# First MLP: the second product moved two slices behind the first, with a third activation buffer and a reordered weight conversion

## The chip, the cores and the metric

The kernel runs on one core of a Trainium2 chip. The metric is device time in microseconds (us) of one execution. The engines are TensorE (PE; its weight loads are listed apart as PEld), VectorE (DVE), ScalarE (ACT), GpSimd (POOL) and SyncE (SP), which here issues every DMA. Each engine runs its own instructions strictly in the order in which they are written, so an instruction that waits holds up all that stand behind it on its engine.

## What is computed

Cross-attention between 512 positions and 32 state rows (8 batches, 8 heads, head size 64) gives 8 x (512 + 32) = 4352 rows of 512. Two MLPs follow, 512 to 2048 to 512 each; the inputs are float32.

```python
xread = softmax(scale * x @ state.T) @ state          # 512 rows per batch
sread = softmax(scale * state @ x.T) @ x              # 32 rows per batch
x = concat([xread, sread])                            # 4352 rows of 512
h = x @ w_in;  g = max(h, 0) + alpha * min(h, 0);  x = g @ w_out      # first MLP
h = x @ w_in2; g = h - tanh(h);                    out = g @ w_out2   # second MLP
```

The weights arrive as 64-bit words and are converted on the core. Each float32 operand of a product is split into a high and a low part, and a product is three matmuls (high x high, high x low, low x high: `TERMS`).

## The kernel before

The first MLP goes through nine blocks of rows: batches 0 to 6, then the small block of all 256 state rows, then batch 7. Each block has 16 slices `f` of 128 hidden columns. For one slice:

- `emit_h` is the **first product**: 12 matmuls of 512 columns in block 0 (weights `wi`), 6 in blocks 1 to 7, where the weights were first multiplied by the state (`pw`), and 12 of 256 columns in the small block. It writes one of two PSUM banks, `ps_h`.
- `act_a` is three steps in a row: ACT writes `t` (L599), DVE rewrites `ps_h` in place from `ps_h` and `t` (L600), ACT writes the high part of `g` (L601). `act_b` is DVE's low part of `g` (L605), the last reader of the `ps_h` bank.
- `emit_o` is the **second product**: 12 matmuls into four accumulators `acc`, which a block holds from its slice 0 to its slice 15. After slice 15 `finish` copies them out to four tiles `y` (two by ACT at L629, two by DVE at L631) and `store` issues their DMAs (L638) at the end of the loop step.

The loop runs the second product one slice late: in step `f` PE gets the first product of `f`, then the second product of `f - 1`. So `finish` of a block falls into step 0 of the next one.

Between these, a timetable written out by hand (`plan`, filled by `at`) places everything else at five points of a step ("early" and "gap" around `act_a`, "mid" ahead of the second product, "late" behind it, "end"): the attention of the next batch, the projections of weights by the state for later blocks (`project`, L367, and `project_one`, L397: three matmuls into `ps_p`, ACT's copy `ph`, DVE's remainder `pl`, and DMAs of both), and, from block 3 on, the conversion and combination of the second MLP's weights (`combining`; stores `wc`). Projections, attention and state transposes share two PSUM banks (`ps_a`). In block 0 the first MLP's own weights are converted: 32 jobs, each half of a pair (w_in of slice f, w_out of slice f), that pass through `conv_load` to `conv_d`, one phase per `tick`; the list `jobs` sets their order. The SBUF pool `work` gives buffers by tag: `g`, `t` and `y` have two each, `sc` and `at` one.

```python
    jobs = [(f, half) for f in range(NF) for half in range(2)]
...
                y = work.tile([P, S], F32, tag="y", name="y")[:, :n]
...
                if pend:
                    emit_o(*pend)
```

Of the kernel before, what the change touches and what calls it, by code (L numbers as in the profile page):

```python
# [12 lines left out]
F32 = mybir.dt.float32  # L13
F32R = mybir.dt.float32r
# [8 lines left out]
P = 128  # L23
# [12 lines left out]
def attention_and_two_mlps(ctx, tc, x, state, w1_in, w1_out, alpha, w2_in, w2_out, out):  # L36
    nc = tc.nc
    B, H, S, D = x.shape
    NS = state.shape[2]
    DM = H * D  # L40
# [3 lines left out]
    NF = DFF // P  # L44
    NC = S // P
    GH = P // NS
    NG = H // GH
    NP = GH // 2
    HP = 2 * NS
    FQ = DM // P  # L50
# [5 lines left out]
    work = tc.alloc_tile_pool(name="work", bufs=2)  # L56
    w_outs = tc.alloc_tile_pool(name="w_outs", bufs=NF // FQ)
# [39 lines left out]
    def w_out(f, part):  # L97
        return WO[f // FQ][:, part, f % FQ, :]
# [22 lines left out]
    def low_word(q, r):  # L121
        nc.scalar.activation(q, r[:, :, 0].bitcast(U32), AF.Copy, scale=2.0**-29)

    jobs = [(f, half) for f in range(NF) for half in range(2)]
    raws, words, low, loaded = {}, {}, {}, set()

    def conv_load(k):
# [160 lines left out]
    xraw, SG = {}, {}  # L288

    def load_state(b, g, tag="sg"):  # L290
        sg = work.tile([P, D], F32, tag=tag, name=f"{tag}{b}_{g}", bufs=4)
        nc.sync.dma_start(out=sg, in_=state[b, g * GH:(g + 1) * GH].rearrange("h n d -> (h n) d"))
        SG[(b, g) if tag == "sg" else (b, g, 0)] = sg

    def load_x(b, g):
        if b < 2:
            load_state(b, g)
        if b == 0:
            if g == 0:
                xraw[b] = w_outs.tile([P, 2 * NC * GH * D], F32, tag="wo", name="xr0")  # L300
            n = NC * GH * D
            t = xraw[b][:, g * n:(g + 1) * n].rearrange("p (c h d) -> p c h d", c=NC, h=GH)
        else:
            t = work.tile([P, NC, GH, D], F32, tag="xr", name=f"xr{b}_{g}")
        for h in range(GH):
            nc.sync.dma_start(out=t[:, :, h, :],
                              in_=x[b, g * GH + h].rearrange("(p c) d -> p c d", c=NC))
        xraw[b, g] = t
# [12 lines left out]
    def lead(b):  # L321
        return b if b % 2 or b == B - 1 else b - 1
# [105 lines left out]
    def attention(b, g, spare=False):  # L428


        st = {}

        def psum(shape, name):
            if spare:
                return ps_acc.tile(shape, F32, tag="acc", name=name)
            return ps_a.tile(shape, F32, tag="a", name=name)

        def wide_tile(tag, other):
            if spare:
                return work.tile([P, S], F32, tag=other, name=tag)  # L440
            return work.tile([P, S], F32, tag=tag, name=tag, bufs=1)

        def transpose_pair(p):
            xr = xraw[b, g]
            ps = psum([P, S], "ps_xt")
            for c in range(NC):
                nc.tensor.transpose(ps[:, c * P:(c + 1) * P], xr[:, c, 2 * p:2 * p + 2, :].rearrange("p h d -> p (h d)"), ident)
            xt = wide_tile("e2t" if p else "e2", "t")
            if b == 0 and p == 1:
                nc.vector.tensor_copy(xt, ps)  # L450
            else:
                nc.scalar.copy(xt, ps)
            st["xt", p] = xt
# [29 lines left out]
            st["s"] = ps  # L483

        def s2t():
            st["sc"] = wide_tile("sc", "y")
            nc.vector.transpose(st["sc"], st["s"])

        def s2b():
            ps = st["s"]  # L490
            mx = work.tile([P, 1], F32, tag="mx2", name="mx2")
            nc.vector.tensor_reduce(mx, ps, axis=AX.X, op=ALU.max)
            nb = work.tile([P, 1], F32, tag="nb", name="nb")
            nc.vector.tensor_scalar(nb, mx, -scale, None, op0=ALU.mult)
            e2 = wide_tile("e2", "t")
            s2_ = work.tile([P, 1], F32, tag="s2", name="s2")
            nc.scalar.activation(e2, ps, AF.Exp, bias=nb, scale=scale, accum_out=s2_)
            st["e2"], st["s2"] = e2, s2_
# [13 lines left out]
        def s3b():  # L512
            ps = ps_a.tile([P, NC, P], F32, tag="a", name="ps_e")
            for c in range(NC):
                nc.tensor.transpose(ps[:, c, :], st["e2"][:, c * P:(c + 1) * P], ident)
            e2t = wide_tile("e2t", "y").rearrange("p (c q) -> p c q", c=NC)
            nc.scalar.copy(e2t, ps)
            st["e2t"] = e2t

# [11 lines left out]
                                    op=ALU.mult)  # L531

        def s4t():
            at = wide_tile("at", "t")
            nc.vector.transpose(at, st["sc"])
            st["at"] = at

# [44 lines left out]
    def emit_h(blk, n, f):  # L582
        ps = ps_h.tile([P, S], F32, tag="h", name="ps_h")
        if 0 < blk < B:
            col = slice(f % FQ * P, (f % FQ + 1) * P)
            pairs = [([PW[blk, f // FQ, g][i][:, col] for i in range(2)], X[0, blk, g]) for g in range(NG)]
        else:
            w = [WS[f][:, i] if blk else w_in(f, i) for i in range(2)]
            pairs = [([w[i][:, cc, :] for i in range(2)], X[0, blk, cc]) for cc in range(NCC)]
        for k, (w, xt) in enumerate(pairs):  # L590
            for m, (i, j) in enumerate(TERMS):
                nc.tensor.matmul(ps[:, :n], lhsT=w[i], rhs=xt[:, j, :n], start=(k == 0 and m == 0),  # L592
                                 stop=(k == len(pairs) - 1 and m == 2))
        return ps[:, :n]

    def act_a(n, f, ph):
        g = work.tile([P, 2, S], F32R, tag="g", name="g")
        t = work.tile([P, S], F32, tag="t", name="t")[:, :n]
        nc.scalar.mul(t, ph, slope[:, f:f + 1])  # L599
        nc.vector.scalar_tensor_tensor(ph, ph, sign[:, f:f + 1], t, op0=ALU.mult, op1=ALU.max)  # L600
        nc.scalar.mul(g[:, 0, :n], ph, sign[:, f:f + 1])  # L601
        return g

    def act_b(n, f, ph, g):
        nc.vector.scalar_tensor_tensor(g[:, 1, :n], ph, sign[:, f:f + 1], g[:, 0, :n].bitcast(F32),  # L605
                                       op0=ALU.mult, op1=ALU.subtract)
# [3 lines left out]
    def emit_o(blk, n, f, g):  # L610
        w = [w_out(f, i) for i in range(2)]
        if f == 0:
            accs[blk] = [ps_acc.tile([P, S], F32, tag="acc", name="acc") for _ in range(NCC)]
        acc = accs[blk]
        for t in range(NCC):
            for k, (i, j) in enumerate(TERMS):
                nc.tensor.matmul(acc[t][:, :n], lhsT=w[i][:, t * P:(t + 1) * P], rhs=g[:, j, :n],  # L617
                                 start=(f == 0 and k == 0), stop=(f == NF - 1 and k == 2))
        if f == NF - 1:
            finish(blk, n, acc)  # L620

    def finish(blk, n, acc):
        for t, a in enumerate(acc):
            if t < 2:
                y = work.tile([P, S], F32, tag="y", name="y")[:, :n]
            else:
                y = work.tile([P, S], F32, tag="sc" if t == 2 else "at", name="y", bufs=1)[:, :n]
            if t % 2 == 0:
                nc.scalar.copy(y, a[:, :n])  # L629
            else:  # L630
                nc.vector.tensor_copy(y, a[:, :n])  # L631
            stores.append((blk, t, y))
# [3 lines left out]
    def store():  # L636
        for blk, t, y in stores:
            nc.sync.dma_start(out=y_dram[blk][t], in_=y)  # L638
        stores.clear()
# [356 lines left out]
    def load_next_x():  # L996
        if nxt[0] < len(groups):
            load_x(*groups[nxt[0]])
            nxt[0] += 1
# [27 lines left out]
    with tc.manual_schedule():  # L1027
# [6 lines left out]
        c = attention(0, 1, spare=True)  # L1034
# [26 lines left out]
        for b in range(2, B):  # L1061
            for g in range(NG):
                i, f = (0, 11) if b == 2 else (b - 2, 6 + 7 * g) if b == lead(b) else (b - 2, 1 + g)
# [74 lines left out]
        for f in range(6, NF):  # L1138
            at(B, f, "late", partial(fill.go, 1))

        pend = None
        for i, (blk, n) in enumerate(seq):
            for f in range(NF):
                ph = emit_h(blk, n, f)
                for z in plan.get((i, f, "early"), ()):
                    z()
                g = act_a(n, f, ph)
                for z in plan.get((i, f, "gap"), ()):
                    z()
                if 0 < i < B:  # L1150
                    act_b(n, f, ph, g)
                for z in plan.get((i, f, "mid"), ()):
                    z()
                if not 0 < i < B:
                    act_b(n, f, ph, g)
                if pend:
                    emit_o(*pend)
                for z in plan.get((i, f, "late"), ()):
                    z()
                pend = (blk, n, f, g)  # L1160
                for z in plan.get((i, f, "end"), ()):
                    z()
                store()
        emit_o(*pend)
        store()

        w_outs.release()
# [113 lines left out]
```

## Time and profile before

| | |
|---|---|
| time of the runs | 1521.59 us, median of 3 (1519.95 to 1524.21) |
| the profiled execution's own time | 1515.88 us |
| its span, first to last instruction | 1514.1 us |
| busy share of the span | PE 94%, PEld 79%, DVE 66%, ACT 49%, POOL 35% |
| first MLP within the span | 27 to about 821 us |

Of the span PE is busy for 1427.2 us. An instruction's start and length are given in us from the start of the span; behind it stands in square brackets how long its engine sat idle before it and whose result ended that wait.

### The profile page before, as it was taken

The numbers are of one execution on the slowest core, as the hardware profiler recorded it, in microseconds if no ns is written. First come the engines' busy times: TensorE is split into PE (matmuls) and PEld (weight loads), VectorE is DVE, ScalarE is ACT, GpSimd is POOL, SyncE is SP. The second block draws the span as 40 slices with busy tenths as digits, with TensorE's granted clock in tenths as the row PEclk, the third lists the DMA queues.
The fourth block names the chain that finished last, engine by engine and source line by source line (L and its number), as shares of the span: only waits on it lengthen the run. The fifth ranks groups of instructions, "written<-read, shape, count | busy, mean of one in ns | idle before, by whom it ended". The sixth has DMA issues, their size and how long they took to land.

```text
span 1514.1 us, 22896 instructions
## 1 busy us (share of the span) xinstructions
PE 1427.2 (94%) x8200; PEld 1191.9 (79%) x8200; DVE 999.5 (66%) x1442; ACT 740.0 (49%) x1338; POOL 533.0 (35%) x414
## 2 busy tenths in 40 slices
PE   6778889999999999998999899999999999999998
PEld 3556666777777677777887787878888989999998
DVE  6988566556576667675345555646347689788884
ACT  4756454444455555554434454545345444444443
POOL 2665100000054444545400121112016487566662
PEclk8988999999999999999999999999999999999999
DMA  6442355875767787759973756272795944343421
GB/s 171 141 137 75 99 152 171 302 224 168 187 193 224 190 245 204 230 179 278 296 222 122 264 203 252 104 272 105 265 348 201 341 133 140 132 140 133 140 85 36
DMA packets 225505, 283.91 MB, mean 188 GB/s; under 512 B 57456, under 2 KB 133232, under 8 KB 224368
## 3 DMA queue, kind: packets, MB, share of 16 engines
q1 hardware_dynamic: 225392, 282.46, 58.3%
q8 instruction: 64, 1.05, 0.3%
q14 instruction: 49, 0.40, 0.1%
HBM read 165.49 MB, written 116.92 MB: 187 GB/s over the span
## 4 chain that ended last, share of the span: by engine, by line
PE 59%; DVE 6%; DMA 6%; ACT 4%; issue 3%; POOL 2%; SPq 1%; ACTq 0%; DVEq 0%; POOLq 0%
PE ps_m L972 21%; PE ps_m L791 16%; PE acc L617 12%; PE ps_h L592 6%; PE ps_p L397 2%; PE ps_m L856 2%; DVE ps_h L600 1%; DMA wc<-c_o 1%; DVE g L605 1%; DMA g<-t 1%; ACT g L601 1%; DMA rx<-y 1%; ACT t L599 1%; DVE c L808 1%; DMA gt<-g 1%
## 5 line engine op out<-in xcount | busy, mean ns | idle before, releaser
L617 PE MATMUL acc<-g,wo 128*128 128x512 f32 (+1 forms) x1728 | 422.5, 392 | 24.0 <-DVE g L605 10.2
L617 PEld LDWEIGHTS acc<-g,wo 128*128 128x128 f32 x1728 | 315.9, 193 | 108.6 <-DVE g L605 17.0
L972 PE MATMUL ps_m<-wp,s 128*128 128x256 f32 x2856 | 342.9, 282 | 2.9 <-ACT e L955 2.8
L972 PEld LDWEIGHTS ps_m<-wp,s 128*128 128x128 f32 x2856 | 341.3, 190 | 4.6 <-ACT e L955 3.2
L791 PE MATMUL ps_m<-x,ch 128*128 128x512 f32 x1344 | 312.4, 394 | 8.8 <-DVE c L808 4.8
L791 PEld LDWEIGHTS ps_m<-x,ch 128*128 128x128 f32 x1344 | 251.8, 188 | 68.9 <-DVE c L808 6.8
L917 DVE TENSOR_TENSOR s<-gt,s 128x512 fp32r<-128x512 f32 (+1 forms) x216 | 217.4, 1058 | 44.3 <-ACT s L933 43.2
L600 DVE SCALAR_TENSOR_TENSOR ps_h<-ps_h,sign,t 128x512 f32<-128x512 f32 (+1 forms) x144 | 104.6, 727 | 134.8 <-ACT t L599 134.5
L592 PE MATMUL ps_h<-x,pw 128*128 128x512 f32 x672 | 176.2, 398 | 0.0
L601 ACT ACTIVATE g<-ps_h,sign 128x512 fp32r<-128x512 f32 (+1 forms) x144 | 95.8, 666 | 161.5 <-DVE ps_h L600 161.5
L933 ACT CAST s<-gt 128x512 fp32r<-128x512 f32 (+1 forms) x216 | 120.4, 597 | 93.3 <-PE ps_m L972 37.1
L217 POOL TENSOR_TENSOR c_q<-c_m,c_q 128x512 int32<-128x512 int32 x32 | 42.1, 1317 | 323.9 <-DMA xr<-in_x 258.9
L605 DVE SCALAR_TENSOR_TENSOR g<-ps_h,sign,g 128x512 fp32r<-128x512 f32 (+1 forms) x144 | 102.6, 713 | 64.1 <-ACT g L601 60.7
L592 PEld LDWEIGHTS ps_h<-x,pw 128*128 128x128 f32 x672 | 123.7, 189 | 27.1
L599 ACT ACTIVATE t<-ps_h,slope 128x512 f32<-128x512 f32 (+1 forms) x144 | 95.9, 666 | 80.7 <-PE ps_h L592 80.3
L802 POOL TENSOR_TENSOR t<-c,t 128x512 f32<-128x512 f32 x32 | 41.7, 1303 | 252.1 <-ACT t L801 226.8
L801 ACT ACTIVATE t<-c 128x512 f32<-128x512 f32 x96 | 60.5, 632 | 124.3 <-DVE c L808 113.8
L808 DVE TENSOR_TENSOR c<-ps_m,c 128x512 f32<-128x512 f32 x96 | 64.7, 684 | 58.7 <-PE ps_m L791 50.3
L244 POOL TENSOR_TENSOR c_o<-c_q,c_o 128x512 fp32r<-128x512 f32 (+1 forms) x48 | 53.7, 1118 | 96.1 <-ACT c_o L242 96.0
L802 DVE TENSOR_TENSOR t<-c,t 128x512 f32<-128x512 f32 x64 | 53.9, 843 | 46.6 <-ACT t L801 45.9
L899 POOL TENSOR_TENSOR s<-gt,gt 128x512 f32<-128x512 f32 (+1 forms) x36 | 52.9, 1474 | 84.5 <-DMA gt<-g 84.1
L797 ACT COPY c<-ps_m 128x512 f32<-128x512 f32 x96 | 55.7, 590 | 39.3 <-PE ps_m L791 28.3
(137 smaller groups left out, 1642.7 us busy)
## 6 DMA issues: line engine op xcount, KB each, us to landing
g<-t SPq DMA_DIRECT2D x128, 256.0 KB, 2.3
gt<-g SPq DMA_DIRECT2D x64, 512.0 KB, 5.4
wc<-c_o SPq DMA_DIRECT2D x112, 256.0 KB, 3.7
ch<-wc SPq DMA_DIRECT2D x56, 512.0 KB, 8.1
pw<-pw SPq DMA_DIRECT2D x96, 256.0 KB, 4.9
wp<-wc SPq DMA_DIRECT2D x28, 512.0 KB, 7.3
xr<-in_x SPq DMA_DIRECT2D x64, 128.0 KB, 3.2
raw<-in_moe_w_in SPq DMA_DIRECT2D x16, 512.0 KB, 3.9
```

Source lines behind the costliest of these rows:

```text
L592: nc.tensor.matmul(ps[:, :n], lhsT=w[i], rhs=xt[:, j, :n], start=(k == 0 and m == 0), stop=(k == len(pairs) - 1 and m == 2))
L599: nc.scalar.mul(t, ph, slope[:, f:f + 1])
L600: nc.vector.scalar_tensor_tensor(ph, ph, sign[:, f:f + 1], t, op0=ALU.mult, op1=ALU.max)
L601: nc.scalar.mul(g[:, 0, :n], ph, sign[:, f:f + 1])
L605: nc.vector.scalar_tensor_tensor(g[:, 1, :n], ph, sign[:, f:f + 1], g[:, 0, :n].bitcast(F32), op0=ALU.mult, op1=ALU.subtract)
L617: nc.tensor.matmul(acc[t][:, :n], lhsT=w[i][:, t * P:(t + 1) * P], rhs=g[:, j, :n], start=(f == 0 and k == 0), stop=(f == NF - 1 and k == 2))
L791: nc.tensor.matmul(b, lhsT=w[p][:, cc], rhs=XT[key, i][cc][:, q], start=(i not in GOES_ON and cc == k == 0), stop=(cc == 1 and k == 2), sk ...
L802: eng.tensor_tensor(t, h, t, op=ALU.subtract)
L808: nc.vector.tensor_tensor(h, ps[j, i], h, op=ALU.add)
L917: nc.vector.tensor_tensor(made[k - 1][:, 1], src, made[k - 1][:, 0].bitcast(F32), op=ALU.subtract)
L933: nc.scalar.copy(made[k][:, 0], source(blk, i, jj))
L972: nc.tensor.matmul(dst[:, t * HW:(t + 1) * HW], lhsT=s[:, p, r, t * P:(t + 1) * P], rhs=w[:, q], start=first, stop=(jj == NJ // 2 - 1 and ...
```

## The change

Four things are edited. `pend` becomes a queue, so that in step `f` PE gets the second product of `f - 2`. The tag `g` gets a third buffer. To make room, `y` no longer has a tag of its own: the first two `y` tiles of a block take buffers of the tag `t`; and the scratch tiles of batch 0's second head group, which used `t` and `y`, now lie in the unused half of the tile `xr0`. Last, `jobs` is reordered: w_in of the slices 0 and 1 come first, and w_out of a slice two places later against w_in.

```diff
-    jobs = [(f, half) for f in range(NF) for half in range(2)]
+    jobs = [(f, 0) for f in range(2)] + [j for f in range(NF) for j in ((f + 2, 0), (f, 1)) if j[0] < NF]
...
-                xraw[b] = w_outs.tile([P, 2 * NC * GH * D], F32, tag="wo", name="xr0")
+                xraw[b] = w_outs.tile([P, 2 * FQ * DM], F32, tag="wo", name="xr0")
...
         def wide_tile(tag, other):
             if spare:
-                return work.tile([P, S], F32, tag=other, name=tag)
+                return xraw[0][:, (NG * NP + other) * S:(NG * NP + other + 1) * S]
             return work.tile([P, S], F32, tag=tag, name=tag, bufs=1)
...
     def act_a(n, f, ph):
-        g = work.tile([P, 2, S], F32R, tag="g", name="g")
+        g = work.tile([P, 2, S], F32R, tag="g", name="g", bufs=3)
         t = work.tile([P, S], F32, tag="t", name="t")[:, :n]
...
     def finish(blk, n, acc):
         for t, a in enumerate(acc):
             if t < 2:
-                y = work.tile([P, S], F32, tag="y", name="y")[:, :n]
+                y = work.tile([P, S], F32, tag="t", name="y")[:, :n]
...
-        pend = None
+        pend = deque()
...
-                if pend:
-                    emit_o(*pend)
+                if len(pend) == 2:
+                    emit_o(*pend.popleft())
...
-                pend = (blk, n, f, g)
+                pend.append((blk, n, f, g))
...
-        emit_o(*pend)
+        while pend:
+            emit_o(*pend.popleft())
```

What moves on PE, in block 0 from its slice 11 on. Before (`g_1183` is the activation of slice 10, `ps_w` a transpose of the attention, `ps_p` a projection for block 1):

```order
L592 MATMUL ps_h_1243<-x0_0_3_376,wi8_847 128x512 x3
L570 MATMUL ps_w_1256<-ident_90,wide_1022 128x128
L617 MATMUL acc_522<-g_1183,wo8_873 128x512 x3
L617 MATMUL acc_523<-g_1183,wo8_873 128x512 x3
L617 MATMUL acc_524<-g_1183,wo8_873 128x512 x3
L617 MATMUL acc_525<-g_1183,wo8_873 128x512 x3
L367 MATMUL ps_p_1302<-wi0_340,snp_694 64x512 x3
L367 MATMUL ps_p_1303<-wi0_340,snp_694 64x512 x3
L592 MATMUL ps_h_1315<-x0_0_0_348,wi12_1166 128x512 x3
```

The same place in the changed kernel (`g_1090` is the activation of slice 9, `g_1165` that of slice 10):

```order
L593 MATMUL ps_h_1225<-x0_0_3_371,wi8_774 128x512 x3
L571 MATMUL ps_w_1238<-ident_90,wide_1004 128x128
L618 MATMUL acc_620<-g_1090,wo8_924 128x512 x3
L618 MATMUL acc_621<-g_1090,wo8_924 128x512 x3
L618 MATMUL acc_622<-g_1090,wo8_924 128x512 x3
L618 MATMUL acc_623<-g_1090,wo8_924 128x512 x3
L368 MATMUL ps_p_1284<-wi0_337,snp_675 64x512 x3
L368 MATMUL ps_p_1285<-wi0_337,snp_675 64x512 x3
L593 MATMUL ps_h_1297<-x0_0_0_344,wi12_1104 128x512 x3
```

Only the slice whose `g` the second product reads has changed; first products and the rest stand where they stood.

On ACT, at the start of block 3 (its steps 0 and 1 before, 1 and 2 after), with what each instruction waits for (DMAHW is the completion of a DMA). Before:

```order
L629 COPY y<-acc 128x512 [waits PE_49] x2
L400 CAST ph<-ps_p 64x512 [waits DMAHW5_49,PE_49,Activation_49]
L599 ACTIVATE t<-ps_h,slope 128x512 [waits PE_49]
L601 ACTIVATE g<-ps_h,sign 128x512 [waits DVE_49]
L400 CAST ph<-ps_p 64x512 [waits DMAHW7_49,PE_49,Activation_49]
```

After:

```order
L630 COPY y<-acc 128x512 [waits PE_49,Activation_49]
L630 COPY y<-acc 128x512 [waits PE_49]
L401 CAST ph<-ps_p 64x512 [waits DMAHW5_49,PE_49,Activation_49]
L600 ACTIVATE t<-ps_h,slope 128x512 [waits DMAHW5_49,PE_49,Activation_49]
L602 ACTIVATE g<-ps_h,sign 128x512 [waits DVE_49]
L401 CAST ph<-ps_p 64x512 [waits DMAHW7_49,PE_49]
L401 CAST ph<-ps_p 64x512 [waits DMAHW1_49,PE_49]
L600 ACTIVATE t<-ps_h,slope 128x512 [waits DMAHW6_49,PE_49]
```

The copies to `y` stand one step later, and `t` of the steps 2 and 3 now waits for a DMA each: the stores of the first two `y` tiles, whose buffers it takes. That is so at each of the eight changes of block.

On SP, around the same four stores. Before, they stand behind the projection stores of step 0 and ahead of those of step 1 (`pw_1_1`):

```order
L403 DMA pw_0_1_130<-pl 64x512 [waits DMAHW0_49,DVE_49]
L638 DMA y_83<-y 128x512 [waits DMAHW1_49]
L638 DMA y_83<-y 128x512 [waits DMAHW2_49]
L638 DMA y_83<-y 128x512 [waits DMAHW3_49]
L638 DMA y_83<-y 128x512 [waits DMAHW4_49]
L403 DMA pw_1_1_132<-ph 64x512 [waits DMAHW5_49,Activation_49]
```

After:

```order
L404 DMA pw_1_1_132<-ph 64x512 [waits DMAHW3_49,Activation_49]
L404 DMA pw_1_1_132<-pl 64x512 [waits DMAHW4_49,DVE_49]
L639 DMA y_83<-y 128x512 [waits DMAHW5_49]
L639 DMA y_83<-y 128x512 [waits DMAHW6_49]
L639 DMA y_83<-y 128x512 [waits DMAHW7_49]
L639 DMA y_83<-y 128x512 [waits DMAHW0_49]
L404 DMA pw_2_1_134<-ph 64x512 [waits DMAHW1_49,Activation_49]
```

The `y` stores now stand behind the projection stores of step 1, which wait for ACT and DVE; in the later blocks it is `wc` stores, which wait for POOL, that come in between.

## Rows read from the trace of the kernel before

**Rows 1.** The page's costliest groups: busy us, mean ns, idle before, releaser.

```profile
L617 PE MATMUL acc<-g,wo 128*128 128x512 f32 (+1 forms) x1728 | 422.5, 392 | 24.0 <-DVE g L605 10.2
```

**Rows 2.** PE's waits in block 0 (27 to 165 us): total, times, longest.

```profile
PE acc L617 <- DVE g L605: 7.2, 2, 3.9
```

**Rows 3.** PE's waits in blocks 2 to 6 (268 to 689 us).

```profile
PE acc L617 <- ACT g L601: 4.5, 8, 1.1
PE acc L617 <- DVE g L605: 2.5, 7, 0.4
```

**Rows 4.** PE's waits in the small block (689 to 751 us).

```profile
PE acc L617 <- ACT g L601: 5.4, 6, 1.7
```

**Rows 5.** Three stretches: length; PE, PEld, DVE, ACT, POOL busy; granted clock, DMA share, GB/s.

```profile
39.00:165.00 126.00, 104.97 (x525) 79.13 (x523) 111.93 (x159) 75.62 (x135) 74.22 (x56) 0.89 0.36 108
134.00:141.00 7.00, 6.97 (x18) 4.66 (x19) 6.83 (x12) 2.81 (x6) 4.65 (x4) 0.58 0.23 55
689.00:751.00 62.00, 53.89 (x375) 49.15 (x374) 31.58 (x56) 30.32 (x64) 34.74 (x34) 0.94 0.98 300
```

**Rows 6.** Timeline of all engines, steps 2 to 4 of block 4.

```profile
469.36 1.30 SPq L246 DMA_DIRECT2D wc<-c_o  x2
470.64 0.69 ACT L599 ACTIVATE t<-ps_h,slope 128x512 f32<-128x512 f32 x1
...
472.88 0.75 DVE L605 SCALAR_TENSOR_TENSOR g<-ps_h,sign,g 128x512 fp32r<-128x512 f32 x1 [0.76 <-ACT g L601]
...
478.45 0.94 PE L592 MATMUL ps_h<-x,pw 128*128 128x512 f32 x3
```

**Rows 7.** Timeline of PE, end of block 0: start, length, instruction, idle before.

```profile
134.00 5.06 PE L617 MATMUL acc<-g,wo 128*128 128x512 f32 x11 [3.87 <-DVE g L605]
138.86 2.29 PE L367 MATMUL ps_p<-wi,snp 128*64 128x512 f32 x6
...
143.80 2.89 PE L617 MATMUL acc<-g,wo 128*128 128x512 f32 x12
146.53 1.55 PE L367 MATMUL ps_p<-wi,snp 128*64 128x512 f32 x6
```

**Rows 8.** DVE's waits from 140 to 165 us.

```profile
DVE ps_h L600 <- ACT t L599: 3.8, 3, 1.6
```

**Rows 9.** Timeline of all engines, steps 1 and 2 of block 3.

```profile
388.48 0.45 SPq L403 DMA_DIRECT2D pw<-pl  x1
388.50 0.69 ACT L599 ACTIVATE t<-ps_h,slope 128x512 f32<-128x512 f32 x1 [0.77 <-PE ps_h L592]
...
391.40 0.67 DVE L401 TENSOR_TENSOR pl<-ps_p,ph 64x512 fp32r<-64x512 f32 x1
...
392.96 0.85 PE L397 MATMUL ps_p<-wi,snp 128*64 128x512 f32 x3
```

**Rows 10.** The four `y` stores after block 2, from issue to landing (374 to 396 us).

```profile
DMA to landing us min/median/max: 3.3/4.1/4.3
```

**Rows 11.** The four `y` stores after block 0 (165 to 190 us).

```profile
DMA to landing us min/median/max: 2.5/2.7/3.0
```

**Rows 12.** The four `y` stores after block 1 (268 to 296 us).

```profile
DMA to landing us min/median/max: 5.7/6.3/6.8
```

**Rows 13.** Timeline of all engines, steps 1 to 4 of the small block.

```profile
701.15 3.23 SPq L638 DMA_DIRECT2D y<-y  x4
...
705.19 0.46 ACT L599 ACTIVATE t<-ps_h,slope 128x256 f32<-128x256 f32 x1
...
706.57 0.60 SPq L246 DMA_DIRECT2D wc<-c_o  x1
706.72 0.48 DVE L605 SCALAR_TENSOR_TENSOR g<-ps_h,sign,g 128x256 fp32r<-128x256 f32 x1 [0.54 <-ACT g L601]
...
708.67 1.57 PE L592 MATMUL ps_h<-x,ws 128*128 128x256 f32 x12
```

**Rows 14.** The four `y` stores after block 6 (694 to 712 us).

```profile
DMA to landing us min/median/max: 5.9/6.4/6.7
```

More of the change, by code (lines that the diff above doesn't have):

```diff
@@ L447, in transpose_pair @@
                 nc.tensor.transpose(ps[:, c * P:(c + 1) * P], xr[:, c, 2 * p:2 * p + 2, :].rearrange("p h d -> p (h d)"), ident)
-            xt = wide_tile("e2t" if p else "e2", "t")
+            xt = wide_tile("e2t" if p else "e2", p)
             if b == 0 and p == 1:
@@ L485, in s2t @@
         def s2t():
-            st["sc"] = wide_tile("sc", "y")
+            st["sc"] = wide_tile("sc", 2)
             nc.vector.transpose(st["sc"], st["s"])
@@ L494, in s2b @@
             nc.vector.tensor_scalar(nb, mx, -scale, None, op0=ALU.mult)
-            e2 = wide_tile("e2", "t")
+            e2 = wide_tile("e2", 0)
             s2_ = work.tile([P, 1], F32, tag="s2", name="s2")
@@ L515, in s3b @@
                 nc.tensor.transpose(ps[:, c, :], st["e2"][:, c * P:(c + 1) * P], ident)
-            e2t = wide_tile("e2t", "y").rearrange("p (c q) -> p c q", c=NC)
+            e2t = wide_tile("e2t", 3).rearrange("p (c q) -> p c q", c=NC)
             nc.scalar.copy(e2t, ps)
@@ L533, in s4t @@
         def s4t():
-            at = wide_tile("at", "t")
+            at = wide_tile("at", 1)
             nc.vector.transpose(at, st["sc"])
```

## The prediction

> **What bounds the kernel now.** I read the page's groups first. In the first MLP PE is the busy engine, and the second product's matmuls are where it idles by name: 24.0 us before them in all, mostly for DVE's `g` [rows 1]. That is the whole prize, so the next view is PE's waits, stage by stage, to see which of them end on `g`. In block 0 they are 7.2 us, in two waits [rows 2]; in blocks 2 to 6 they are 4.5 and 2.5 us, many waits of at most 1.1 us [rows 3]; in the small block 5.4 us [rows 4]. Block 1 and the last block have next to none. The third view is the table of stretches: in block 0 DVE is busy for 111.93 of 126 us, so DVE sets the pace there and PE's waits are partly its shadow; in the small block the granted clock is 0.94, in block 0 0.89, so part of the time PE runs at 1.2 GHz instead of 2.4 [rows 5].
>
> **What the change gives.** The number of instructions stays: the same matmuls, copies and stores, the same 32 conversion jobs. What a second product gains is a first and a second product more between its `g` and itself. Its new neighbour is the `ps_h` bank: there are two, so the first product of f + 2 waits for `act_b` of f, which comes one second product earlier than the need for `g` did. From `t` to the end of `act_b` the chain takes 470.64 to 472.88 + 0.75, 3.0 us [rows 6], against a second, a first and a second product ahead of that bank's next use (2.8 + 1.4 + 2.8, about 7): hidden, with some 4 to 5 us to spare.
>
> (a) Blocks 2 to 6: all 7.0 us [rows 3] go. (b) Small block: one of the six waits lies ahead of the stall found below, so five sixths of 5.4, 4.5 us [rows 4]. (c) Block 0: at 134.00 PE has waited 3.87 us for DVE, and then runs the second product (11 matmuls in 5.06 us) and the projection (2.29) to 143.80, where the next second product starts [rows 7]. With the change it fills the wait with an older second product and the projection, and at 134.00 has a first product (141.15 to 143.80, 2.7 us) and a second (2.89) left: it reaches the same point 4.2 us sooner. But DVE, whose work is unchanged, must gain it too: from there to the block's end it waits 3.8 us for `t` [rows 8]. I take 3.8. The earlier wait of block 0 falls where DVE has no gap to give, and counts nothing. The lower bound of (c) is 0, if DVE's gaps stay. (d) Clock of the small block: 0.94 over 62 us [rows 5] means 7.4 us at half speed, which cost up to 3.7; half, 1.9. Sum 17.2 us; bounds 10 and 19.
>
> The new order of `jobs` and the moved scratch tiles I cost at nothing. The jobs pass DVE, ACT and POOL in the same places of their queues, w_in now earlier and w_out one place later for a consumer one step later; DVE covers it, being full [rows 5]. If that cover were gone, a late w_out would show as PE waiting on a weight tile `wo`, of which there is none now.
>
> **What the change costs.** `y` now takes `t`'s buffers, so at each of the eight changes of block `t` of step 2 (and, later and with less effect, of step 3) waits until a store to DRAM has landed. ACT is in order: behind `t` stand its high part of `g`, the projection copies `ph` and the attention's copies, and behind those DVE and PE.
>
> Into block 3: the first `y` store can go out once the projection store of step 1 has (388.48 + 0.45), at 389.0 [rows 9], and such stores took 4.1 us there [rows 10]: 393.1. `t` started at 388.50: 4.6 us late. From `t` to the end of the projection's `pl` in step 2 it is 388.50 to 391.40 + 0.67, 3.6 us, so `pl` ends at 396.7. PE needs that bank for its next `ps_p` at 392.96 [rows 9], since the scores of the attention hold the other: a stall of **3.7 us**. Read the same way, the changes into blocks 1 and 2, which have projections too, give 3.8 and 3.6. Together 11.1. With landings of 2.5 us [rows 11] it is 6.2; with 6.8 [rows 12] about 19.
>
> Into block 4, without projections: the store goes behind two `wc` stores, at 470.7, lands 6.3 later [rows 12], at 477.0, and `act_b` of step 2 ends 3.0 us on, at 480.0; the first product of step 4 would start at 478.45 [rows 6]: **1.6 us**. The changes into blocks 5 and 6 read the same way give 2.5 and 0.3. Together 4.4; bounds 0 and 6.
>
> Into the small block: the store goes behind the `wc` at 706.57 + 0.60, less the 3.23 us that the `y` stores now take ahead of it, so at 703.9 [rows 13], lands 6.4 later [rows 14], 710.3, and `act_b` ends 2.0 us after `t`'s start (705.19 to 707.20), at 712.3, where the first product of step 4 stood at 708.67 [rows 13]: **3.6 us**; bounds 0 and 4. Into the last block nothing stands between copy and store: 0.
>
> Clock: behind the 3.87 us wait of block 0 the granted clock is 0.58 for 7 us [rows 5], and the second product and the projection take 5.06 and 2.29 instead of 2.89 and 1.55 [rows 7]: 2.9 us more. Four of the new stalls are about as long. I take half of it for each, 5.8 us; bounds 0 and 11.6.
>
> The costs sum to 11.1 + 4.4 + 3.6 + 5.8 = 24.9 us, against 17.2 gained: **7.7 us slower**, 1523.6 us for the profiled execution of 1515.88. That execution lies 5.7 us under the median of the runs, 1521.59, and on the median's scale the forecast is **1529 us**.
>
> **The landing time decides, and a rule speaks to it.** The trace has 2.5 to 3.0 us at the first change of block [rows 11], 4.1 at the third [rows 10], 6.3 and 6.4 at two others [rows 12, 14]. The Trainium skill, "DMA: Bandwidth & Descriptors", section "Anatomy of one DMA", fits a transfer as about 2.0 us fixed, mostly the receipt of the last write, plus its bytes at 436 GB/s; that is an estimate of 2.6 us for these 256 KB. The trace agrees at the first change only, and by the page the sum would be that of the first rival.
>
> **The rivals.** *Stores that land quickly* (faster): if all land in 2.5 us, as after block 0 [rows 11], the costs are 6.2 us of projection stalls, nothing in the other blocks and no clock, so 17.2 - 6.2 = 11 us faster, 1511. For it: the `y` stores move to another moment, with other transfers ahead. Against it: in four of the shown cases they took longer. My sum has them at 5.0 us on average; between the two it is linear, and it turns at about 4.0 us.
>
> *Even*: costs and gains cancel within 0.3%. For it: both sums are about 20 us and independent. 0.3% is 4.6 us, about what a measurement of this kernel can tell from no change.
>
> *Stalls that compound* (much slower): all three projection stalls with landings as after block 1 (2.2 us more each, 17.7), the whole clock loss of 11.6, the rest as above: 37.3 - 17.2, 20 us slower, 1542. For it: ACT has to work off what piled up behind `t` while DMAs in the small block are at a share of 0.98 [rows 5]. Against it: ACT is half idle elsewhere.
>
> *The change doesn't do what it says*: the bank `ps_h` could hold PE where `g` did. The 7 us against 3.0 speak against it; its price is the gain, and it adds to the slow cases.
>
> **How the numbers follow.** Forecast 0.38 (own range 1523 to 1535; a sixth of it within 0.3%), quick stores 0.25, even 0.20, compounding with the last rival 0.17. Slower 0.32 + 0.17 = 0.49, same 0.26, faster 0.25. The range reaches from the quick stores to just short of the compounded case, 1511 to 1541.
>
> **What the profile after would show.** ACT's waits: `t` on the DMA of `y`, 16 times, some 35 to 40 us in all, a new row at the top; if it is under 15 us, the first rival holds. PE's waits on `g` gone but for the changes of block; in their place three waits of 3 to 4 us of `ps_p` for `pl` in the first steps of blocks 1 to 3, and one of the first product in the small block for DVE. Block 0 shorter by about 4 us with unchanged DVE time; the stretch of blocks 2 to 6 no shorter, though its `g` waits are gone. I am wrong if PE's stalls at the changes of block sum to less than half of 19 us, or if block 0 gains more than DVE's 3.8.

## The result and the profile after

The changed kernel takes 1539.37 us (median of 6 runs, 1528.45 to 1540.25) beside 1520.8 us of the kernel before in the same comparison: a ratio of 1.0112, with a 95% interval of 1.008 to 1.0144. It is slower by 1.1%, some 17 us, where 0.5% was forecast. The profiled execution took 1540.13 us, its span is 1538.4 us, 24.3 us more than before. PE's busy time is 1429.1 us beside 1427.2: what grew in sum is PE's idle time.

First the page's costliest groups (busy us, mean ns | idle us just before them, and what ended most of it), which answer [rows 1]; the line numbers of the changed kernel are one higher from the first MLP on:

```profile
L618 PE MATMUL acc<-g,wo 128*128 128x512 f32 (+1 forms) x1728 | 410.5, 387 | 0.0
L593 PE MATMUL ps_h<-x,pw 128*128 128x512 f32 x672 | 180.7, 405 | 4.8 <-DMA pw<-pw 4.2
```

The 24.0 us of idle time before the second product are gone to the last tenth. The change did what it says, and the kernel is slower all the same. So the next view is ACT's waits over the whole span, where the prediction wanted a new row:

```profile
ACT t L600 <- DMA y<-y: 28.6, 7, 7.0
```

There it is: seven waits of `t` for a `y` store to land, up to 7.0 us. To see what each is worth I take the start of `t` in step 0 of each block from the timelines; the difference of two such starts is the length of a block (block 7 is the small one; the last length goes from step 0 to step 15). The rows e1 to e11 are the experiments below.

```
block               0      1      2      3      4      5      6    7 (small)  8    all
before            136.7  104.6  103.0   84.9   77.5   77.1   79.6   58.9   60.3  782.4
after             140.2  110.2  109.1   85.4   79.8   74.8   77.3   60.6   65.1  802.7
e1 (y out of t)   138.0  105.8  105.2   81.7   76.6   71.6   76.8   58.8   61.9  776.2
e7 (and more)     139.5  104.3  107.8   81.9   76.6   71.6   77.1   57.0   58.8  774.6
e8 (e7, one lag)  137.6  105.7  109.7   84.4   77.5   77.1   77.0   59.6   60.4  788.9
e11               138.6  104.9  105.3   82.6   76.6   71.6   76.8   58.0   58.8  773.1
```

With a lag of two, one second product of 2.9 us more and one of 1.6 us less fall into the small block's stretch, and the reverse into the last one's: 1.3 us that say nothing. Block 0's stretch holds one second product, 2.9 us of PE's work, less, and at the table's end that one is still to come. Every stage but blocks 5 and 6 is longer than before: blocks 0 to 2 by 3.5, 5.6 and 6.1 us, the last by 4.8.

The first change of block, on all engines (the start in us, the length, the engine and line, and in brackets the idle time before and what ended it):

```profile
181.10 1.09 ACT L630 COPY y<-acc 128x512 f32<-128x512 f32 x2
...
187.43 0.58 SPq L418 DMA_DIRECT2D wi<-wi  x1
188.06 3.88 SPq L639 DMA_DIRECT2D y<-y  x4
...
192.49 0.69 ACT L600 ACTIVATE t<-ps_h,slope 128x512 f32<-128x512 f32 x1 [6.99 <-DMA y<-y]
193.21 0.76 DVE L601 SCALAR_TENSOR_TENSOR ps_h<-ps_h,sign,t 128x512 f32<-128x512 f32 x1 [6.87 <-ACT t L600]
...
195.51 0.68 DVE L382 TENSOR_TENSOR pl<-ps_p,ph 64x512 fp32r<-64x512 f32 x1
...
196.25 1.54 PE L368 MATMUL ps_p<-wi,snp 128*64 128x512 f32 x3 [5.76 <-DVE pl L382]
```

Read it as a chain: the copy of `y` is done at 182.2, but its store stands in SP's queue behind projection stores and a load and is issued only at 188.06; ACT, which has stood still for 6.99 us, writes `t` at 192.49, as soon as the first of the four has landed; the projection's `ph` and `pl` stand behind, and PE has waited 5.76 us for `pl` (1.5 us at the same place in the kernel before). From the end of the copy to `t` it is 10.3 us: 5.9 in SP's queue, and 4.4 from the issue on.

The small block, answering to [rows 13]:

```profile
712.67 1.17 ACT L630 COPY y<-acc 128x512 f32<-128x512 f32 x2
...
714.55 2.77 SPq L427 DMA_DIRECT2D ws<-wi  x2
...
717.42 1.51 SPq L247 DMA_DIRECT2D wc<-c_o  x1
...
719.03 2.50 SPq L639 DMA_DIRECT2D y<-y  x4
719.10 0.67 ACT L112 ACTIVATE c_m<-c_raw 128x512 f32<-128x512 f32 x1 [5.27 <-DMA c_raw<-in_moe_w_out]
...
724.78 0.47 ACT L600 ACTIVATE t<-ps_h,slope 128x256 f32<-128x256 f32 x1 [5.01 <-DMA y<-y]
...
726.86 2.93 PE L593 MATMUL ps_h<-x,ws 128*128 128x256 f32 x12 [7.28 <-DVE g L606]
```

The same chain, with a store that is issued 5.2 us behind the copies and takes 5.7 us until `t` goes (up to 719.10 ACT waits for a load, `c_raw`, as well); PE's first product stands still for 7.28 us, and runs for 2.93 us instead of 1.57 behind it.

The last block has a stall that nothing in [rows 1 to 14] hints at:

```profile
774.75 2.16 SPq L639 DMA_DIRECT2D y<-y  x4
...
776.96 2.01 SPq L698 DMA_DIRECT2D rx<-y  x4
...
779.01 6.02 SPq L686 DMA_DIRECT2D ch<-wc  x7
...
785.92 12.64 SPq L411 DMA_DIRECT2D pw<-pw  x8
...
800.30 1.23 PE L593 MATMUL ps_h<-x,pw 128*128 128x512 f32 x3 [2.10 <-DMA pw<-pw]
802.51 1.62 PE L593 MATMUL ps_h<-x,pw 128*128 128x512 f32 x3 [0.98 <-DMA pw<-pw]
803.93 4.62 PE L618 MATMUL acc<-g,wo 128*128 128x512 f32 x12
```

The `y` stores of the small block now come a step later, eleven loads of 512 KB for the second MLP (`rx`, `ch`) stand behind them on SP, and the weights `pw` of the block's third quarter behind those. The first four, issued from 785.92 on, took 12.4 to 13.1 us to land among those loads, and PE waits for them, and runs the next second product in 4.62 instead of 2.88 us.

Last, PE's waits in block 0 (27 to 165 us: total us, times, longest), answering to [rows 2]:

```profile
PE ps_e L516 <- ACT e L498: 6.9, 2, 6.2
PE ps_p L368 <- DVE xw L574: 6.6, 1, 6.6
PE ps_st L336 <- DVE sm L328: 3.9, 1, 3.9
PE ps_st L336 <- DVE xw L574: 3.7, 1, 3.7
```

The same rows in the kernel before:

```profile
PE ps_e L515 <- ACT e L497: 4.5, 2, 3.8
PE ps_st L335 <- DVE sm L327: 3.7, 1, 3.7
PE ps_st L335 <- DVE xw L573: 2.2, 1, 2.2
```

The waits on `g` have gone. The wait of `ps_p` for `xw` is new, and three that were there before are longer: PE's idle time in block 0 rose from 24.8 to 32.9 us, in a stretch that holds a second product of 2.9 us less.

### The profile page after: what moved, and what is told of

It reads as the page before. It is cut to its first block, busy times and chain, and to the rows that moved or that the text cites. A ratio compares the mean times of both kernels' runs of the same rounds, so it can differ in the third digit from the quotient of the medians.

```text
span 1538.4 us, 22919 instructions
## 1 busy us (share of the span) xinstructions
PE 1429.1 (93%) x8200; PEld 1197.6 (78%) x8200; DVE 1001.1 (65%) x1442; ACT 739.5 (48%) x1338; POOL 532.8 (35%) x414
## 3 DMA queue, kind: packets, MB, share of 16 engines
q8 instruction: 65, 1.06, 0.3%
## 4 chain that ended last, share of the span: by engine, by line
PE 59%; DMA 7%; DVE 5%; ACT 3%; issue 2%; SPq 1%; POOL 1%; ACTq 0%; DVEq 0%; POOLq 0%
PE ps_m L973 20%; PE ps_m L792 17%; PE acc L618 12%; PE ps_h L593 6%; PE ps_p L398 2%; PE ps_m L857 2%; DMA pw<-pw 1%; DVE ps_h L601 1%; DMA ch<-wc 1%; DVE g L606 1%; DMA y<-y 1%; ACT g L602 1%; DMA rx<-y 1%; DMA wp<-wc 1%; DMA gt<-g 1%
## 5 line engine op out<-in xcount | busy, mean ns | idle before, releaser
L618 PE MATMUL acc<-g,wo 128*128 128x512 f32 (+1 forms) x1728 | 410.5, 387 | 0.0
L601 DVE SCALAR_TENSOR_TENSOR ps_h<-ps_h,sign,t 128x512 f32<-128x512 f32 (+1 forms) x144 | 104.7, 727 | 159.2 <-ACT t L600 158.7
L593 PE MATMUL ps_h<-x,pw 128*128 128x512 f32 x672 | 180.7, 405 | 4.8 <-DMA pw<-pw 4.2
```

## The experiments

Theory A: the loss is the shared buffer, `t` waiting for `y` to land. Theory B: the loss lies in the lag itself (copies, stores and projections a step later). All ratios are to the kernel before, run on the same chip. Its median was 1516.0 to 1518.0 us there, 3 to 5 us below the 1520.8 of the result, and a time that was expected from the result's runs comes out lower by as much.

**e1: `y` out of `t`'s buffers.**

```diff
-                y = work.tile([P, S], F32, tag="t", name="y")[:, :n]
+                y = work.tile([P, S], F32, tag="cq" if t else "cm", name="y", bufs=3)[:, :n]
```

> The changed kernel, but y of the first two tiles no longer takes the buffers of t: it takes those of the conversion's and projection's scratch (cm, cq; three each). Theory A (t waits for the landing of the y stores, and that is the loss): ACT's wait of t on y, 28.6 us in 7 waits, is gone, and with it the jumps of 2.9 to 9.6 us at the changes into blocks 1, 2, 3 and the small block; 3 us of block 0 and about 6 us in the last block stay: 1510 to 1522 us. Theory B (the loss is the lag itself: y copied and stored a step later, the projection waiting for DVE, the loads behind the y stores late): 1532 to 1540 us.

1517.4 us, ratio 1.0006 (0.9989 to 1.0023). ACT's `t` has no wait for `y` left. The whole loss is gone, and A holds. As a whole e1 is even with the kernel before; what the lag is worth by itself this doesn't tell, since e1 keeps PE's waits for `pw` in the last block (4.3 us) and has block 2 longer by 2.2 us (see e7 and e8).

**e2: the shared buffer without the lag.** The second product one slice behind, two buffers of `g`, the old `jobs`.

```diff
-    jobs = [(f, 0) for f in range(2)] + [j for f in range(NF) for j in ((f + 2, 0), (f, 1)) if j[0] < NF]
+    jobs = [(f, half) for f in range(NF) for half in range(2)]
...
-        g = work.tile([P, 2, S], F32R, tag="g", name="g", bufs=3)
+        g = work.tile([P, 2, S], F32R, tag="g", name="g")
...
-                if len(pend) == 2:
+                if len(pend) == 1:
```

> The second product one slice behind, two buffers of g and the old order of jobs, as before the change; only y in the buffers of t and the scratch tiles in xraw as in the changed kernel. Theory A: t waits for y at the changes of block, here from step 1, 20 to 35 us in sum on ACT, and the time is 1533 to 1546 us. Theory B: 1517 to 1525 us, as before the change.

1546.76 us, ratio 1.0208 (1.0192 to 1.0224), and ACT's row is longer than in the changed kernel:

```profile
ACT t L600 <- DMA y<-y: 42.4, 8, 10.5
```

The time is at the upper end of what was expected (1533 to 1546 us), ACT's wait above it (20 to 35). Without the lag the shared buffer (with the moved scratch tiles, which no run has alone) costs 2.1%, twice what the whole change costs. With the lag of two, the third `g` and the new `jobs` it is about half; why, no run separates.

**e3: the order of `jobs` alone**, in the kernel before.

```diff
-    jobs = [(f, half) for f in range(NF) for half in range(2)]
+    jobs = [(f, 0) for f in range(2)] + [j for f in range(NF) for j in ((f + 2, 0), (f, 1)) if j[0] < NF]
```

> The kernel before with the new order of jobs alone. Theory A, in which the jobs cost nothing: 1517 to 1525 us, block 0 of the same length within 1 us. If the order of jobs is what made block 0 longer by 3 us instead of shorter by 3.8: 1523 to 1528 us, block 0 3 us longer.

1515.66 us, ratio 1.0004 (0.9992 to 1.0016); block 0 is 136.9 us long beside 136.7. It costs nothing that can be measured.

**e5: the `y` stores right behind the second product.**

```diff
                 if len(pend) == 2:
                     emit_o(*pend.popleft())
+                store()
                 for z in plan.get((i, f, "late"), ()):
```

> The changed kernel with the y stores issued right behind the last second product of a block, ahead of the step's late work (projection stores, loads, wc stores). If the wait of t is mostly the stores' place in SP's queue (issue 3 to 7 us behind the copy): ACT's wait of t on y falls from 28.6 to about 10 to 15 us, and the time to 1522 to 1532 us. If it is mostly the landing itself (4.0 us in the middle): the wait stays above 20 us and the time at 1533 to 1541.

1525.8 us, ratio 1.0071 (1.0056 to 1.0086); the row has come down to

```profile
ACT t L600 <- DMA y<-y: 19.0, 7, 5.6
```

That is more than the 10 to 15 us expected, while the time is where it was expected. At the first change of block, where 5.9 of 10.3 us lay ahead of the issue, the wait is gone; in the small block it is not (5.6 us), since a `wc` store is still ahead. The place in SP's queue is about a third of the wait, and by the ratios, whose intervals just overlap, some 6 us (1.0112 less 1.0071) of the time.

**e6: the loads for the second MLP two steps later**, behind the weights.

```diff
-        at(B, 2, "late", open_slots)
+        at(B, 4, "late", open_slots)
```

> The changed kernel with the eleven loads for the second MLP (rx, ch; 5.5 MB) issued at step 4 of the last block, behind the weights of its third quarter, instead of at step 2, ahead of them. If the last block's stall comes from these weights standing behind those loads, which stand behind the y stores of a step later: PE's waits for pw, 4.2 us in three, are gone, the last block is 66 to 67 us long instead of 71.1, and the time is 1533 to 1536 us. If the weights are late for another reason (their buffer): the waits stay and the time is 1537 to 1541.

1530.48 us (1533 to 1536 were expected; the kernel before took 1515.99 here), ratio 1.0093 (1.0066 to 1.0121). The last block's waits for `pw` are gone, and its stretch is 58.8 us instead of 65.1. The trace shows the mechanism; by the ratios, whose intervals overlap, it is worth some 3 us.

**e7 and e8: the value of the lag by itself.** e7 is the changed kernel with the edits of e1, e5 and e6. e8 is e7 with one line back at a lag of one:

```diff
-                if len(pend) == 2:
+                if len(pend) == 1:
```

> Two slices of lag with the three side effects taken away: y out of t's buffers (as in e1), y stores right behind the second product (as in e5), the loads for the second MLP behind the weights (as in e6). Theory A (the lag itself is worth the waits on g in blocks 2 to 6, some 7 us; block 0 and the small block give nothing): 1509 to 1514 us beside 1516.5 of before. If the lag is worth nothing at all: 1516 to 1520.

> The same with the second product one slice behind, and nothing else changed: the value of the lag by itself. Theory A: PE's waits on g are back (some 15 to 22 us in the first MLP), but block 0 and the small block are as long as with two slices, so it is 5 to 9 us slower than the run with two: 1515 to 1521. If the lag is worth nothing: within 2 us of it. If the lag costs by itself (later y, later projection): faster than it.

e7: 1515.7 us, ratio 0.9986 (0.9973 to 0.9999), some 2 us over what was expected. e8: 1521.67 us, ratio 1.0026 (1.0011 to 1.004). So the lag is worth 6 us here (their one profiled execution each is 14 us apart, which the medians don't bear out). At a lag of one, e8 is slower than the kernel before by 0.26%: `y`'s new place or another of its edits has a price of its own, and block 2, 109.7 us for 103.0, is where the traces show it. Page groups of e7, then of e8:

```profile
L618 PE MATMUL acc<-g,wo 128*128 128x512 f32 (+1 forms) x1728 | 407.9, 386 | 0.0
```

```profile
L618 PE MATMUL acc<-g,wo 128*128 128x512 f32 (+1 forms) x1728 | 420.0, 391 | 24.4 <-ACT g L602 11.2
```

Besides the 24.4 us of waits, the second product's busy time falls by 12.1 us. And still only 6 us of time come of it: the waits come back elsewhere. Over the first MLP PE is idle for 62.1 us in e7 and 64.8 in e8. In the small block (PE's waits, e7 from 689 to 747 us, then e8 from 700 to 760):

```profile
PE ps_h L593 <- DVE g L606: 7.3, 6, 2.1
```

```profile
PE acc L618 <- ACT g L602: 6.6, 7, 2.8
```

The same idle time stands under another name: at a lag of two the first product waits for its bank, which `act_b` still reads. What the small block gains (57.0 beside 59.6 us) is not idle time, 7.3 beside 7.5 us of its stretch, but busy time (last section).

e7's table also shows a jump that is left, block 2 with 107.8 us instead of 103.0. On ACT, at the change from block 1:

```profile
287.56 1.07 ACT L630 COPY y<-acc 128x512 f32<-128x512 f32 x2 [3.65 <-DMA pw<-ph]
```

It is the same fault the other way round: `y` now waits for a projection store, whose `ph` holds the buffer of `cm`.

**e9: that jump.** e7, and at that one change of block `y` takes the third buffer of `g`.

```diff
+        pair = work.tile([P, 2, S], F32, tag="g", name="y2", bufs=3) if blk == 1 else None
         for t, a in enumerate(acc):
-            if t < 2:
+            if t < 2 and blk == 1:
+                y = pair[:, t, :n]
+            elif t < 2:
```

> The run e7 with one thing changed: at the change from block 1 to block 2, y's first two tiles take the third buffer of g instead of the projection's cm and cq. If e7's jump there (4.6 us, the projection's copies waiting for the y stores) is such a buffer wait again: it goes, but for 1 to 2 us since g of step 2 then waits for a second product; 1511 to 1514 us beside e7's 1515.7. If it is the DMA or the SP queue: no change.

1513.76 us, ratio 0.9976 (0.9961 to 0.9991). Block 2 is 104.4 us long; between steps 1 and 3 its starts lose 1.5 us against the kernel before, where e7's lose 4.8. The trace shows the wait gone; the two ratios, whose intervals overlap, can't tell it in the time.

**e10: block 0's projections a step later**, in e7.

```diff
-            at(0, 11 + g, "late", partial(project, 1, 0, g, (0,)))
+            at(0, 12 + g, "late", partial(project, 1, 0, g, (0,)))
```

> The run e7 with the two projections of block 0 at steps 12 and 13 instead of 11 and 12. If the projection, whose PSUM banks DVE's xw and ACT's e hold, is what keeps the lag from gaining in block 0: PE's wait for xw (6.6 us) goes and block 0 is 2 to 4 us shorter. If DVE's own work sets block 0's length, whatever PE has to fill in: the wait moves to the ps_h bank or the transposes, and block 0 keeps its length within 1 us.

1515.73 us, ratio 0.9985 (0.9966 to 1.0003), as e7. PE's wait of 6.6 us for `xw` is gone; new in its place (27 to 165 us):

```profile
PE ps_e L516 <- DVE pw L382: 4.9, 1, 4.9
...
PE ps_h L593 <- DVE g L606: 4.0, 2, 2.4
```

Block 0 is 142.3 us long beside 139.5. The wait moves, the block is no shorter: neither expectation quite, but the second one's mechanism.

**e11: a lag of one in block 0, of two behind it**, in e9.

```diff
-                if len(pend) == 2:
+                if len(pend) == (2 if i else 1):
```

> The run e9 with the second product one slice behind in block 0 and two from block 1 on. If the lag itself costs block 0 some 2 to 4 us (the second product that filled PE's wait has moved ahead of it, and PE then idles longer, with a lower clock behind it): block 0 is as long as before the change (within 0.7 us) and the time 1510 to 1513 us. If block 0's 1 to 4 us in these runs are scatter of DVE's pace: no change from e9, 1512 to 1515.

1510.4 us beside 1517.97 of the kernel before, ratio 0.995 (0.9932 to 0.9968): faster than the kernel before, and by the ratio than e9, though the two intervals just overlap. PE's idle time in block 0 is 28.4 us beside 33.0 in e9, whose stretch holds a second product less. Its length is 138.6 us, not the 136.7 expected: over all runs block 0 is 136.7 to 139.6 us long at a lag of one there (five runs) and 138.0 to 141.2 at two (six, e10 aside).

## Why the prediction came out as it did

The direction and the range held (1511 to 1541, the median 1.6 us below its upper end); the size did not, 17 us by the ratio where the sum had 7.7. The four stalls named in advance did come, 5.8, 3.8, 2.0 and 7.3 us of PE; a block 0 shorter by 4 us did not, it is 3.5 us longer.

**The costs were about right in sum.** The sum has 24.9 us. Between the changed kernel and e1, which differ in nothing but `y`'s place, lie 1.06% of ratio, 16 us, and in the traces of the first MLP 26.5 us (802.7 and 776.2; e1's profiled execution is the fastest of its twelve, 5.6 us below their median). Of these, 17.7 us are idle time of PE (82.4 and 64.6), where the stalls of the sum are 19.1. The mechanism and its places were those written down: `t` on the store of `y`, then `ph`, `pl`, and PE's `ps_p`. The projection stalls were 5.8, 3.8 and 2.0 us for 3.8, 3.6 and 3.7, 11.6 for 11.1 in sum, though 1.5 of the 5.8 stood there before the change. PE's waits over the whole span, the second row with a third wait of 0.2 us:

```profile
PE ps_p L368 <- DVE pl L382: 5.8, 1, 5.8
PE ps_p L398 <- DVE pl L402: 6.0, 3, 3.8
```

ACT's wait was 28.6 us for 35 to 40, in 7 waits for 16: the second `t` of a change of block never waits for its store. Into the small block 3.6 us was too little for 7.28: the store was taken to be issued at 703.9, and with the 10 us by which the kernel was then late (`t` of step 1 at 711.26 instead of 701.30), that is 714, but it went at 719.03, behind two `ws` loads and a `wc` store. Into the last block the sum has 0 because "nothing stands between copy and store"; what stands *behind* the store in SP's queue was not looked at, and that is the stall on `pw`. e1 has it too, so it comes of the store's later step and not of the shared buffer.

**The clock term was too small.** The sum has 5.8 us lost behind the new stalls, with bounds of 0 and 11.6, and 1.9 gained in the small block. Half speed did follow the stalls (the second product in the last block at 4.62 instead of 2.88 us, the small block at a granted clock of 0.92 beside 0.94). Between e1 and the changed kernel, with the same matmuls in the same order, PE's busy time in the first MLP rises from 711.6 to 720.3 us, 8.8 us, at a granted clock of 0.97 and 0.96; over the whole span the pages have, e1 first:

```profile
PE 1417.4 (94%) x8200; PEld 1190.6 (79%) x8200; DVE 1000.4 (66%) x1442; ACT 738.5 (49%) x1338; POOL 532.8 (35%) x414
PE 1429.1 (93%) x8200; PEld 1197.6 (78%) x8200; DVE 1001.1 (65%) x1442; ACT 739.5 (48%) x1338; POOL 532.8 (35%) x414
```

Against the kernel before, PE's busy time is up by only 1.9 us, as the second product's runs fell by 12 us at the same time, which no term had (last section). The 1.9 us of the small block can't be told from scatter: its granted clock is 0.94 in the kernel before and 1.00 in e3, whose PE order is the same.

**The landing time**, on which the first rival hung, was not the short one: `y` stores took 4.3 us at the first change of block and 5.5 us in the small block, 4.0 in the middle of all. The fit of the Trainium skill, "DMA: Bandwidth & Descriptors", section "Anatomy of one DMA", which that section gives for DMAs issued by GpSimd while these are issued by SyncE, makes an estimate of 2.6 us for 256 KB; the trace agrees at two changes of block alone (2.4 to 3.0 us into block 3, 2.0 to 2.7 into block 6) and has 3.6 to 5.7 us at the others that store 256 KB. (In the kernel before, too, the first change was not the only quick one: into block 6 it was 2.7 to 3.2 us.) And e5 shows that a part of the wait was no landing at all but the place in the queue.

**The gains failed, by two of their steps, (b) and (c).** They sum to 17.2 us; e7 against e8 puts them at 6 us, and in e1, with the wait for `pw` and the longer block 2 against them, nothing is left.

(c) Block 0, 3.8 us: "With the change it fills the wait with an older second product and the projection". The projection couldn't fill it. Its two PSUM banks are the ones that DVE's `xw` and ACT's `e` had still to read, and DVE does `xw` 4.5 us behind the `g` that PE used to wait for. With the second product moved ahead, PE had nothing at all there, idled 6.61 us instead of 3.87, and ran the next first product in 4.07 us instead of 2.98:

```profile
134.62 0.74 DVE L606 SCALAR_TENSOR_TENSOR g<-ps_h,sign,g 128x512 fp32r<-128x512 f32 x1
...
139.08 0.25 DVE L574 TENSOR_REDUCE xw<-ps_w 128x64 f32<-128x128 f32 x1
...
139.38 1.54 PE L368 MATMUL ps_p<-wi,snp 128*64 128x512 f32 x3 [6.61 <-DVE xw L574]
...
142.97 4.07 PE L593 MATMUL ps_h<-x,wi 128*128 128x512 f32 x12
```

DVE, as the prediction said of the upper bound, has to gain too, and it did not. e11 against e9 puts the lag in block 0 at a loss of 0.26%, 4 us, with intervals that just overlap.

(b) The small block, 4.5 us: the wait on `g` went, and the same 7 us came back as a wait for the `ps_h` bank (e7). The prediction had priced that rival with the 7 us that lie ahead of the bank's next use in a big block; with 256 columns the products are half as long (1.6 us), while ACT's queue (conversion copies, loads awaited) is not. That this makes the difference is read from the trace and not tested.

(a) Blocks 2 to 6, 7.0 us: right, and mis-sized downward. In e1 these five blocks take 411.9 us beside 422.1, though block 2 is 2.2 us longer there. PE's idle time in them is 11.5 us beside 17.3; the rest of the 10.2 us is busy time (last section).

So the forecast had its direction from costs that were about right, and its size wrong by gains that mostly were not there; that the range held all the same is owed to its width. What stays open: the traces of the first MLP make e7 11 us better than e8 (14 in the table, less the product still to come), the medians 6, and one profiled execution of each can't tell where the rest went.

## What to carry to other kernels

Where two tiles share a buffer, ask how its last reader gets done: here DVE's pass over `t` took 0.76 us, while a store of `y` landed 2.0 to 5.7 us after its issue, and at the first change of block was issued only 5.9 us behind the copy. Put such a tile where the next writer is several steps away, and look at what stands behind the store as well as ahead of it. And before counting a wait that a deeper pipeline removes as a gain, look for the next thing on the same engine that the same late engine must free: in a stage that another engine sets, the wait only changes its name.

## What the runs showed that was not expected

Part of a wait can stand in the list as busy time. With all waits on `g` gone, the same 1728 matmuls of the second product are busy for 407.9 instead of 420.0 us (e7 and e8, mean granted clock 0.981 and 0.982). Where some of it sits is plain in the small block, here PE's timeline of e3, which has the lag of one:

```profile
711.56 2.10 PE L617 MATMUL acc<-g,wo 128*128 128x256 f32 x12 [0.84 <-ACT g L601]
...
719.26 1.60 PE L617 MATMUL acc<-g,wo 128*128 128x256 f32 x12
```

Each of the five second products that follow a wait between 700 and 733 us took 2.09 or 2.10 us, each of the others 1.60, at a granted clock of 1.00 throughout. It looks as if the matmuls themselves were slower behind a wait, but the weight loads of the first of these two show a second wait inside the row:

```profile
711.56 0.19 PEld L617 LDWEIGHTS acc<-g,wo 128*128 128x128 f32 x1 [1.05 <-ACT g L601]
712.08 1.02 PEld L617 LDWEIGHTS acc<-g,wo 128*128 128x128 f32 x8 [0.33 <-DVE g L605]
```

The first matmul takes the high part of `g`, which ACT writes (L601); the second takes the low part, which DVE has only ready half a microsecond later (L605). So the second matmul starts 0.52 us behind the first, where 0.12 us is the spacing in a run without waits: 0.40 of the 0.50 us is a wait for DVE, of which only 0.13 count as idle time of PE. The other 0.1 us lies between the second matmul and the third; no run says why. Worked out from the starts in e8, 16 second products have both waits at full clock and are 0.37 us longer each than those without, some 6 of the 12.1 us; some 4 more lie in those that ran partly at half speed (seven in e8, five in e7). A wait on the first part of a two-part operand is thus worth more than its row in the list of waits.
